# One rounding step of an attention kernel may run on GpSimd, and the written-out order behind the first batch is another one

## The chip, the cores and the metric

The kernel runs on one core of a Trainium2 chip. The metric is the time of one execution on the device in microseconds (us). A core has five engines with a queue of instructions each: TensorE (PE in the profile, its weight loads PEld), VectorE (DVE), ScalarE (ACT), GpSimd (POOL) and SyncE (SP), which here does nothing but issue DMAs. Each queue is worked off in order; engines wait for each other through semaphores.

## The reference

Block-causal attention over 8 batches with 8 heads, 576 tokens and 64 columns a head, then a two-layer feed-forward net with a relu6 gate:

```python
scores = scale * np.matmul(q, k.transpose(0, 1, 3, 2))          # q, k, v: (8, 8, 576, 64)
mask = block_i >= block_j                                        # blocks of 64 tokens
attn = exp(where(mask, scores, -1e9) - max); attn /= attn.sum() + 1e-9
x = (attn @ v).transpose(0, 2, 1, 3).reshape(4608, 512)
h = x @ w_in                                                     # 512 x 2048
g = h * np.clip(h + 3.0, 0.0, 6.0) / 6.0
out = g @ w_out                                                  # 2048 x 512
```

## The kernel before

**Numbers.** Behind the first batch every product is made of float16 words: a float32 value is split into a high word and a low word (the rest), and a product is three matmuls: high times high, high times low, low times high. So each intermediate needs two steps that round: one that writes the high word (`scaled`, on ACT or DVE), and one that computes value times scale minus high word (a `scalar_tensor_tensor` on DVE).

**Attention.** Two heads of a batch form a slot `n` (32 slots; 0 to 3 are the first batch, which is computed in float32). `qk_prep` splits q and k into the tile `qks`, and a transposing DMA brings it to `qkT`. `s_group(n, g)` does three blocks of 64 query rows: score matmuls into PSUM (`s`), a DVE step that moves them to `p` and takes the extreme value, the exponential on ACT, one divided by the sum in `st`, and then the split of P into the tiles `phl`. Query block `i` has 64 (i + 1) columns, so every block with an even `i` ends in a half block of 64 columns (five of nine blocks, 140 over slots 4 to 31). Where there are full columns besides, GpSimd first clears the other half of the last unit (`MEMSET p`). The high word of the half block goes into the left half of the last unit of `phl`, its low word into the right half. SP then issues a transposing DMA from `phl` to `pT` (five a slot), and the matmuls `pv` read `pT`.

**Feed-forward net.** 13 pieces of 384 tokens: `h` (x times w_in), relu6 and split into `g`, `o` (g times w_out). The last pieces use a seven-product scheme on half-size blocks: `w_comb` (tiles `wr`, `wq`, `ws`), `x_comb` (`xr`, `xt`) and `t_comb` (`tr`, `tw`) form sums and differences of the weights and of x, the products are `m`, and `g_pair` forms sums and differences of g in the tile `rs` and splits them into `gs` and `gr`, which the last `o` matmuls read. Sums and differences of `wr`, `xr`, `tr`, `tw` and `rs` may be done by DVE or by GpSimd.

**Order.** Nothing is scheduled when the kernel runs. The program is recorded as 6612 steps (`Recorder.add`, with the ways in which engines can do a step), and the table `ORDER` says in which order the steps are issued and on which engine each runs; `SLOTS` says which buffer of a pool each tile takes. `emit` plays the table, at one line for all engines: L423 before, L425 in the changed kernel.

Of the kernel before, what the change touches and what calls it, by code (L numbers as in the profile page):

```python
# [24 lines left out]
U = 2.211  # L25
# [58 lines left out]
    "%oBEx1`Qsn7?7C2QU(rmb#{wa(XnjzbcUrzT;r*er^gjO>DzDe<KQeIZ(hbzX;8A2yi_)9{Df@dip-{vi4ny`lSCzA375kcj2L-1"
    "yt!snN?zoU(PL&NrRuKaF3K+m3SOL+6Qv*97CmL<{#h}x#|*RU8>cF+wzMv3Dk~2?6BZJ>blLj$Yj9z%AFrrXTZeUYEmv!%byjWI"
    "xUaXmc4GJQIdwe^FQ(5RpW0Msd*Y<#*YC-v56pd7f8of{M}I!S#ku(S$-zUD{@yS%zZC!F^1P>*&u_ZppS_yDdyn?(%eSjn^{h!q"
    "tf^gVadVvw*0O=Q?e&ijtgTx%Z~tcXJ*oMpQpI-POQE&2PPx_g&Vyrzx4!$)v%lBy0WJjMxbc18Pw(SaI$_Yv+jj;J={NM=Fr2qG"
    "ynT6xD}BbS`?@nLR!+;!Ti_2xFv<qTC2)OL`S=Cs4J4}l&fY7DNduEp@^@V=C`_KWJ2Gm%vGYj!)Yxka7aYsHe)M>GT2WTTNKxgO"
# [1852 lines left out]
```

## Time and profile before

| | |
|---|---|
| runs | median 953.36 us (952.73 to 955.15, three runs) |
| the profiled execution | 951.95 us, its span 950.2 us |
| PE busy | 942.8 us of the span |
| DVE busy | 860.0 us |
| ACT busy | 722.0 us |
| POOL busy | 98.3 us |

An engine's busy time is the time in which its profiled instructions ran; the rest of the span it waited. The profiled execution's own time is 1.75 us above its span, which is what lies before the first and behind the last instruction.

### The profile page before, as it was taken

Reading aid. Unit: us, or ns where it says so; the run is one execution under the profiler, and the core shown is the slowest. Engines: PE = TensorE matmul, PEld = TensorE weight load, DVE = VectorE, ACT = ScalarE, POOL = GpSimd, SP = SyncE. Lnnn points to the kernel's source line nnn. Section 1 sums busy time; section 2 is a strip of 40 time slices with the busy share of each in tenths; the row PEclk is TensorE's granted clock in tenths of the full one; section 3 lists DMA queues with packets and bytes.
Section 4 is the critical chain, followed back from the end, with each engine's and each line's share of the span. In section 5 each row is a group of like instructions: output and inputs, shape, how many; then the busy total and the mean of one; then the engine's idle time right before and its main releaser. Section 6 shows DMA issues by size and latency. Waiting matters only on the chain.

```text
span 950.2 us, 34711 instructions
## 1 busy us (share of the span) xinstructions
PE 942.8 (99%) x14108; PEld 686.3 (72%) x14108; DVE 860.0 (91%) x2526; ACT 722.0 (76%) x1791; POOL 98.3 (10%) x283
## 2 busy tenths in 40 slices
PE   9999999999999999999999999999999999999998
PEld 7777777766677766666667666666666667789998
DVE  5988999999999999999999999999899998999987
ACT  6989898888988878888788878778665356676662
POOL 1443101100000000110000010100000102000000
PEclk9999999999999999999999999999999999999999
DMA  7877699989999999999999899986785000000001
GB/s 211 280 246 213 125 178 169 180 166 181 167 189 168 179 188 162 183 189 181 165 201 181 169 165 180 179 162 121 127 128 106 2 2 36 2 35 4 14 26 36
DMA packets 390704, 132.93 MB, mean 140 GB/s; under 512 B 373264, under 2 KB 376592, under 8 KB 390544
## 3 DMA queue, kind: packets, MB, share of 16 engines
q1 hardware_dynamic: 389456, 129.87, 71.7%
q8 instruction: 110, 1.80, 0.8%
q10 hardware_dynamic: 1088, 0.85, 0.3%
q14 instruction: 50, 0.41, 0.1%
HBM read 45.09 MB, written 9.44 MB: 57 GB/s over the span
## 4 chain that ended last, share of the span: by engine, by line
PE 97%; DMA 1%; DVE 1%; ACT 0%; issue 0%; SPq 0%; DVEq 0%
PE o L423 37%; PE h L423 30%; PE m L423 9%; PE s L423 7%; PE pv L423 6%; PE pf L423 1%; PE sf L423 1%; PE pt L423 1%; DMA qkT<-qks 1%; PE pr L423 1%; PE gm L423 0%; DMA qf<-in_q_dram 0%; PE warm L423 0%; PE o_1b L423 0%; PE o_2b L423 0%; PE o_0b L423 0%
## 5 line engine op out<-in xcount | busy, mean ns | idle before, releaser
L423 PE MATMUL o<-wout,g 128*64 128x512 f16 (+2 forms) x2760 | 346.5, 378 | 0.0
L423 PE MATMUL h<-x,win 128*64 128x384 f16 (+2 forms) x3568 | 330.1, 318 | 0.0
L423 PEld LDWEIGHTS <-win 128*64 128x64 f16 (+1 forms) x4432 | 231.7, 110 | 81.3 <-issue 1.7
L423 PEld LDWEIGHTS <-g 128*64 128x64 f16 x2784 | 154.0, 110 | 98.6
L423 DVE SCALAR_TENSOR_TENSOR phl<-p,st,phl 128x64 f16<-128x64 f32 (+4 forms) x364 | 154.9, 447 | 4.2 <-ACT phl L423 2.3
L423 ACT ACTIVATE p<-p,st 128x192 f32<-128x192 f32 (+8 forms) x252 | 139.1, 553 | 22.7 <-DVE st L423 20.7
L423 DVE CUSTOM_DVE_ANT_0 p<-s,none,esc 128x64 f32<-128x64 f32 (+7 forms) x252 | 119.9, 486 | 14.6 <-PE s L423 11.2
L423 ACT ACTIVATE r<-h,eg,sh 128x384 f32<-128x384 f32 (+1 forms) x176 | 101.5, 591 | 40.2 <-PE h L423 33.9
L423 ACT ACTIVATE phl<-p,st 128x512 f16<-128x512 f32 (+5 forms) x173 | 97.2, 582 | 11.2 <-DVE st L423 6.1
L423 PE MATMUL s<-qkT 128*64 128x512 f16 (+7 forms) x1120 | 98.5, 287 | 0.8 <-DMA qkT<-qks 0.8
L423 DVE SCALAR_TENSOR_TENSOR g<-r,g 128x384 f16<-128x384 f32 (+1 forms) x160 | 86.2, 546 | 3.8 <-ACT g L423 3.0
L423 DVE SCALAR_TENSOR_TENSOR r<-r,eg,h 128x384 f32<-128x384 f32 (+1 forms) x144 | 84.2, 586 | 5.8 <-ACT r L423 4.5
L423 ACT ACTIVATE g<-r 128x384 f16<-128x384 f32 (+1 forms) x117 | 58.3, 503 | 18.2 <-PE o L423 11.3
L423 PEld LDWEIGHTS <-qkT 128*64 128x64 f16 x1120 | 53.4, 110 | 25.1 <-DMA qkT<-qks 1.0
L423 PEld LDWEIGHTS <-vhl 128*64 128x64 f16 x1344 | 58.4, 110 | 13.4
L423 PE MATMUL pv<-pT,vhl 128*64 128x192 f16 (+2 forms) x1344 | 67.2, 233 | 0.0
L423 ACT ACTIVATE hf<-m 128x192 f32<-128x192 f32 x90 | 28.5, 327 | 36.9 <-PE m L423 31.9
L423 PEld LDWEIGHTS <-ws 128*64 128x64 f16 x1152 | 52.0, 110 | 4.1
L423 ACT ACTIVATION_READ_ACCUMULATOR p<-p,st 128x1 f32 x252 | 47.7, 189 | 0.0
L423 DVE SCALAR_TENSOR_TENSOR qks<-qk,rs_q,qks 128x576 f16<-128x576 f32 x56 | 46.8, 838 | 0.9 <-ACT qks L423 0.6
L423 PE MATMUL m<-x,ws 128*64 128x192 f16 x864 | 46.8, 246 | 0.0
L423 PE MATMUL m<-x,win 128*64 128x192 f16 x768 | 41.4, 246 | 0.4 <-DVE hf L423 0.4
(229 smaller groups left out, 1414.1 us busy)
## 6 DMA issues: line engine op xcount, KB each, us to landing
vx<-vhl SPq DMA_DIRECT2D x56, 160.0 KB, 3.4
vnat<-in_v_dram SPq DMA_DIRECT2D x63, 128.0 KB, 3.5
qk<-in_k_dram SPq DMA_DIRECT2D x28, 288.0 KB, 4.4
qk<-in_q_dram SPq DMA_DIRECT2D x28, 288.0 KB, 3.9
out_dram<-osb SPq DMA_DIRECT2D x29, 256.0 KB, 2.8
rawo<-in_moe_w_out_dram SPq DMA_DIRECT2D x13, 512.0 KB, 4.9
x<-in_moe_w_in_dram SPq DMA_DIRECT2D x9, 512.0 KB, 5.5
rawi<-in_moe_w_in_dram SPq DMA_DIRECT2D x6, 512.0 KB, 4.8
```

Of the source, the lines that this page charges most:

```text
L423: getattr(eng, method)(*args, **kw)
```

## The change

A new way for one step of `s_group`: the low word of a half block was one `scalar_tensor_tensor` on DVE; it may now also be two instructions on GpSimd, a `tensor_scalar` that multiplies the 64 columns of `p` in place by the scale, and a `tensor_tensor` that subtracts the high word. `ORDER` and `SLOTS` are other tables. Steps 0 to 899 of the order are as before, through the first batch; behind it the order differs throughout, and 503 of the 6612 steps run on another engine: 205 go from DVE to GpSimd (102 of the 140 low half blocks, the rest sums and differences), 144 from ACT to DVE, 109 from DVE to ACT, and 45 others.

```diff
--- before.py
+++ after.py
 ORDER = (
-    "c-l>Q1zaNC_qQS{Dvi0Rlyrl-X(u3IZra_oZrk0pZg+QgcXxMpcmL02pWpj=hvCLK-#GWqAk3~ghHbra)#^2C*O9O`!>rbC*obr4"
+    "c-lQ#1wb23(?$XT;t5)X2uX+=QpJKt30B43oht4wE!5rJ-QC^Y-Ch6L^!>k0xZRz3WOnazxwNKcuGp2UR<BvRj)buuVYz<8Mk}XH"
...
 )
 SLOTS = (
...
-    "Dmit$6EbYehQO3tn^m6AJKxerDn5LKB<*kJGQ7^&IkrmUwiEWL^LM6&x$xlkb>AM)%+2XL#wwB!+hKg<r2P*T{516+l#)KS><Op"
+    "=+LzJ%dIA&_PDK`eJZ+jkonGnRj+SWjo8hhITyMm!xr`VcmRARC!O+|O2*4OqkMW%u4F#9EfrTBeiWFBOGD6iJ^<nabCU^@"
 )
...
@@ -1153,9 +1155,14 @@
             else:
                 nc.scaled(ph[:, last, :BLK], pr[:, :BLK], r, "AV")
             if half:
-                nc.vector.scalar_tensor_tensor(
-                    ph[:, last, BLK:], pr[:, nk - BLK:nk], r, ph[:, last, :BLK], op0=ALU.mult, op1=ALU.subtract
-                )
+                ph_, pl, pw_ = ph[:, last, :BLK], ph[:, last, BLK:], pr[:, nk - BLK:nk]
+                nc.add([
+                    ("vector", "scalar_tensor_tensor", (pl, pw_, r, ph_), dict(op0=ALU.mult, op1=ALU.subtract)),
+                    ("gpsimd", [
+                        ("tensor_scalar", (pw_, pw_, r, 1.0), dict(op0=ALU.mult, op1=ALU.mult)),
+                        ("tensor_tensor", (pl, pw_, ph_), dict(op=ALU.subtract)),
+                    ]),
+                ])
             if g == 2:
                 nu = 2 * full + bool(half)
                 t_dma(pT[n, 1][:, BASE[i]:BASE[i] + nu], ph[:, :nu])
```

**GpSimd, behind the first batch.** These are the rows of GpSimd's queue where it first differs, before (a number behind a tile's name is slot and group or block: `p4_2` is block 2 of slot 4):

```order
L423 MEMSET p4_2_531 128x64
L423 MEMSET p4_4_552 128x64
L423 MEMSET phl4_1_555 128x128
L423 TENSOR_SCALAR qks5_541<-qks5_541 128x2x9x32 x2
L423 TENSOR_SCALAR st4_1_548<-st4_1_548 128x3
L423 MEMSET p4_8_582 128x64
L423 TENSOR_SCALAR qks6_609<-qks6_609 128x2x9x32
L423 TENSOR_SCALAR st4_2_577<-st4_2_577 128x3
```

And of the change:

```order
L425 MEMSET p4_2_531 128x64
L425 MEMSET p4_4_552 128x64
L425 MEMSET phl4_1_555 128x128
L425 TENSOR_SCALAR qks5_541<-qks5_541 128x2x9x32 x2
L425 TENSOR_SCALAR p4_2_531<-p4_2_531,st4_0_527 128x64
L425 TENSOR_TENSOR phl4_0_532<-p4_2_531,phl4_0_532 128x64
L425 TENSOR_SCALAR st4_1_548<-st4_1_548 128x3
L425 MEMSET p4_6_581 128x64
L425 TENSOR_SCALAR st4_2_577<-st4_2_577 128x3
L425 MEMSET p4_8_582 128x64
L425 TENSOR_SCALAR p4_8_582<-p4_8_582,st4_2_577 128x64
L425 TENSOR_TENSOR phl4_8_586<-p4_8_582,phl4_8_586 128x64
```

Behind the `MEMSET` of `p4_2` the low word of that block now stands as two rows, and block 8 follows; a `qks` step of slot 6 is gone from this place.

**DVE and GpSimd, late in the feed-forward net.** These are DVE's rows before around the sums `rs11_3` of piece 11 (`hf` is h of that group, `tr5` and `tw5` are combined weights that a later group needs):

```order
L423 SCALAR_TENSOR_TENSOR hf11_3_2392<-rs11_3_2395,eg8_698,hf11_3_2392 128x768
L423 SCALAR_TENSOR_TENSOR gs11_2_1_2391<-rs11_2_2388,gs11_2_1_2391 128x384
L423 TENSOR_TENSOR rs11_3_2395<-hf11_3_2392 128x192
L423 TENSOR_TENSOR hf11_4_2399<-m11_4_26_2401,hf11_4_2399 128x192
L423 TENSOR_TENSOR tr5_1_2344<-wout_86 128x512
L423 TENSOR_TENSOR hf11_4_2399<-m11_4_25_2400,hf11_4_2399 128x192
L423 TENSOR_TENSOR vnat_101<-tw4_2342,vnat_101 128x3x256
L423 TENSOR_TENSOR rs11_3_2395<-rs11_3_2395,hf11_3_2392 128x192
L423 TENSOR_TENSOR tw5_2345<-tr5_0_2343 128x256
L423 TENSOR_TENSOR hf11_4_2399<-m11_4_26_2401,hf11_4_2399 128x192
L423 SCALAR_TENSOR_TENSOR gr11_3_2396<-hf11_3_2392,gr11_3_2396 128x576
L423 TENSOR_TENSOR rs11_3_2395<-hf11_3_2392,rs11_3_2395 128x192
```

DVE's rows of the change at the same place:

```order
L425 SCALAR_TENSOR_TENSOR hf11_3_2392<-rs11_3_2395,eg8_698,hf11_3_2392 128x768
L425 TENSOR_TENSOR rs11_3_2395<-hf11_3_2392 128x192
L425 SCALAR_TENSOR_TENSOR gs11_2_0_2390<-rs11_2_2388,gs11_2_0_2390 128x384
L425 SCALAR_TENSOR_TENSOR gs11_2_1_2391<-rs11_2_2388,gs11_2_1_2391 128x384
L425 TENSOR_TENSOR hf11_4_2399<-m11_4_25_2400,hf11_4_2399 128x192
L425 TENSOR_TENSOR hf11_4_2399<-m11_4_26_2401,hf11_4_2399 128x192 x2
L425 TENSOR_TENSOR vnat_101<-tw4_2342,vnat_101 128x3x256
L425 SCALAR_TENSOR_TENSOR gr11_3_2396<-hf11_3_2392,gr11_3_2396 128x576
L425 SCALAR_TENSOR_TENSOR gs11_3_1_2398<-rs11_3_2395,gs11_3_1_2398 128x384
```

And GpSimd's of the change, of which before had none there:

```order
L425 TENSOR_TENSOR tr5_0_2343<-wout_86 128x512
L425 TENSOR_TENSOR tr5_1_2344<-wout_86 128x512
L425 TENSOR_TENSOR rs11_3_2395<-hf11_3_2392 128x192
L425 TENSOR_TENSOR rs11_3_2395<-rs11_3_2395,hf11_3_2392 128x192
L425 TENSOR_TENSOR rs11_3_2395<-hf11_3_2392,rs11_3_2395 128x192
L425 TENSOR_TENSOR tw5_2345<-tr5_0_2343 128x256
L425 TENSOR_TENSOR tw5_2345<-tr5_1_2344,tw5_2345 128x256
L425 TENSOR_TENSOR rs11_4_2402<-hf11_4_2399 128x192
L425 TENSOR_TENSOR rs11_4_2402<-rs11_4_2402,hf11_4_2399 128x192
L425 TENSOR_TENSOR rs11_4_2402<-hf11_4_2399,rs11_4_2402 128x192
```

One of the four `rs11_3` steps stays on DVE; three go to GpSimd, where they stand behind `tr5` and ahead of `tw5`.

**SP, at one transposing DMA.** These are SP's rows before that lead to `qkT13`:

```order
L423 DMA out_0_dram<-osb2_0_968 128x512
L423 DMA vnat_101<-in_v_dram 128x4x64 x2
L423 DMA_TRANSPOSE pT11_1_1022<-phl11_7_1031 128x8x128
L423 DMA vnat_101<-in_v_dram 128x4x64 x2
L423 DMA_TRANSPOSE pT11_1_1022<-phl11_8_1032 128x9x128
L423 DMA vnat_101<-in_v_dram 64x2x64
L423 DMA_TRANSPOSE qkT13_1069<-qks13_1062 128x27x128
```

And of the change:

```order
L425 DMA_TRANSPOSE pT11_1_1022<-phl11_6_1030 128x7x128
L425 DMA out_0_dram<-osb2_0_968 128x512
L425 DMA_TRANSPOSE pT11_1_1022<-phl11_8_1032 128x9x128
L425 DMA vnat_101<-in_v_dram 64x2x64
L425 DMA vnat_101<-in_v_dram 128x4x64 x2
L425 DMA_TRANSPOSE pT11_1_1022<-phl11_7_1031 128x8x128
L425 DMA_TRANSPOSE qkT13_1069<-qks13_1062 128x27x128
```

The transposing DMA of `qkT13` keeps its row number in the queue; what stands ahead of it changes places, and two DMAs fewer stand between the store of `osb2_0` and it.

## Rows read from the trace of the kernel before

**Rows 1.** The page: span, and busy time of each engine with its count.
```profile
span 950.2 us, 34711 instructions
...
PE 942.8 (99%) x14108; PEld 686.3 (72%) x14108; DVE 860.0 (91%) x2526; ACT 722.0 (76%) x1791; POOL 98.3 (10%) x283
```

**Rows 2.** Waits of PE: engine, tile, releaser; us in total, times, longest.
```profile
PE warm L423 <- DVE zero L423: 1.1, 1, 1.1
PE s L423 <- DMA qkT<-qks: 0.8, 1, 0.8
PE qt L423 <- DMA qf<-in_q_dram: 0.6, 1, 0.6
PE m L423 <- DVE hf L423: 0.4, 1, 0.4
```

**Rows 3.** Busy us by stretch (count): PE, PEld, DVE, ACT, POOL, clock, DMA.
```profile
0.00:50.00 50.00, 48.16 (x618) 36.70 (x619) 35.75 (x131) 38.55 (x110) 16.43 (x44) 1.00 0.76 242
...
150.00:700.00 550.00, 549.20 (x7704) 373.78 (x7702) 507.65 (x1586) 453.42 (x1165) 44.43 (x182) 1.00 0.98 171
700.00:830.00 130.00, 130.00 (x1908) 91.38 (x1906) 118.23 (x267) 73.11 (x153) 12.05 (x14) 1.00 0.21 41
830.00:930.00 100.00, 99.65 (x2286) 95.45 (x2284) 93.01 (x226) 64.13 (x142) 1.31 (x2) 1.00 0.06 19
930.00:950.20 20.20, 15.80 (x378) 15.54 (x373) 14.16 (x35) 2.95 (x6) 0.00 (x0) 0.95 0.15 42
```

**Rows 4.** Timeline of SP ahead of the wait for qkT: start, us.
```profile
293.01 1.54 SPq L423 DMA_TRANSPOSE pT<-phl  x1
294.60 0.67 SPq L423 DMA_DIRECT2D vnat<-in_v_dram  x1
295.37 5.07 SPq L423 DMA_TRANSPOSE qkT<-qks  x1
```

**Rows 5.** Timeline of PE at the same place: start, us.
```profile
298.35 0.91 PE L423 MATMUL pv<-pT,vhl 128*64 128x192 f16 x18
...
302.56 0.53 PE L423 MATMUL s<-qkT 128*64 128x64 f16 x12 [0.81 <-DMA qkT<-qks]
```

**Rows 6.** Groups by form, DVE and ACT: count, busy us, mean ns, idle before.
```profile
L423 DVE SCALAR_TENSOR_TENSOR g<-r,g 128x384 f16<-128x384 f32 x144 | 80.6, 567 | 2.8 <-ACT g L423 2.1
...
L423 ACT ACTIVATE g<-r 128x384 f16<-128x384 f32 x108 | 55.1, 515 | 15.7 <-PE o L423 9.7 <-DVE r L423 4.4 <-DVE st L423 0.9
...
L423 DVE SCALAR_TENSOR_TENSOR phl<-p,st,phl 128x64 f16<-128x64 f32 x140 | 39.2, 284 | 2.4 <-ACT phl L423 1.4
...
L423 DVE TENSOR_SCALAR g<-r 128x384 f16<-128x384 f32 x36 | 12.8, 354 | 1.2 <-PE mb_q L423 0.8
...
L423 DVE TENSOR_TENSOR rs<-hf 128x192 f32<-128x192 f32 x31 | 10.5, 353 | 0.2
```

**Rows 7.** Groups by form of POOL: count, busy us, mean ns, idle before.
```profile
L423 POOL TENSOR_SCALAR qks<-qks 128x576 f16<-128x576 f16 x26 | 20.9, 802 | 71.7 <-DVE qks L423 43.0 <-ACT qks L423 22.9 <-DVE pp L423 3.4
...
L423 POOL TENSOR_SCALAR st<-st 128x3 f32<-128x3 f32 x40 | 10.8, 271 | 230.7 <-ACT p L423 202.7 <-DVE r L423 12.6 <-issue 11.3
...
L423 POOL TENSOR_SCALAR sgi<-x 128x512 int32<-128x512 uint32 x9 | 6.6, 737 | 11.2 <-DVE win L423 3.3 <-DVE rsio L423 2.7 <-DVE wu L423 1.8
...
L423 POOL TENSOR_TENSOR tr<-wout 128x512 f32<-128x512 f16 x1 | 1.2, 1218 | 0.1
L423 POOL TENSOR_TENSOR tw<-tr,tr 128x256 f32<-128x256 f32 x1 | 0.7, 732 | 0.0
L423 POOL TENSOR_TENSOR rs<-hf 128x192 f32<-128x192 f32 x1 | 0.7, 712 | 110.9 <-DVE hf L423 110.9
```

**Rows 8.** Timeline of POOL and DVE at 744 us: start, us.
```profile
744.49 2.18 POOL L423 TENSOR_TENSOR wr<-win 128x1024 f32<-128x1024 f16 x1 [13.52 <-DVE wq L423]
744.71 2.37 DVE L423 SCALAR_TENSOR_TENSOR g<-r,g 128x384 f16<-128x384 f32 x1
```

**Rows 9.** DMA issues: count, us from issue to landing.
```profile
pT<-phl SPq DMA_TRANSPOSE x140, 4.2
```

More of the change, by code (lines that the diff above doesn't have):

```diff
@@ L84 @@
[L84 to L88, printed above, removed]
@@ new lines @@
+    "-HMgjjZHgxcdx47(?>7cnVhnE#>`m<7@Kxg<=nWwkGc2Yo42X^*Ke~sa{JCLdxv9-*Bm;&cJ`c`fANHGzrJrbIdk^G&k4WJ-Mx4J"
+    "o#|29!-<FOY|m3aUHCl7?8}vgtD7%x+4}5{z4^uTukWv=U9ubL^Zdn2-z7_zz4CtjgGBLH63Lzc83X5ju(I~E_p)(tbo%HZk;?ip"
+    "Pv9O689H1(C?TGu2pH__=o05n$GEc77#1F}O{Y$tE-84@f57C&L74)#dFf9jfk~FKQt61Y30dJQGMa-Y8j1=h35!KyE{De-HTtlo"
+    "rFKkmZp5&$<7OtNXs_ff%F7Q7TAZ34sT<!OHD%@gS<x}a^s^h9rpm9jwk>HcuLwC48XU58+4_!aaAK|>udE8ghIV!@4^vI=s@|}1"
+    "UvEv_#GdDK>Zdin=$k=4wW;3b#7Wh!-;+-tnESBd!jYqo{(ORybMf($gNG*ly<uW{DelYVc~8wgzv+p4_G<p_J?gJ7->zOYZB2Ya"
@@ new lines @@
+    "ZQWY)o9nDG7LCkpuYY`CZQZhY`!~z)i7h`B?yl^;6k2QBlw0lZJUBQ!_U=c|fnFmAIT45@W&Pjx^>ZnmFl6TKJ41&J7=CYrmA6{c"
+    "vAolnK4aE>?U@xTr|0A@@P{H8<%476xxTA>{FFL9iE6vE_ew(I;H2cdU03r9lIHD>h@2nZbtG+S%(aCJj%8dwdb}dFFtc*Buxi}c"
+    "G2@FiUfR4R%dNVmc++LWu&*h5_NIRmL|?c#inn^r_6OZ3*RDIUHR>^c-}l+VAE#0d96Y^a&fG(XfByRYXWQ^wf*UvAEPQ)={f57H"
+    "vTv3xzI*T8{Ra;p85WtbvTWa9&z>-e$LETc<P6H~@6>O=zzA1c<zQ!*C;L?<cA}-6OTLlfT8TI>zW^&8G4Ux|=4NBcbU%_=6JkX_"
+    "y6l++L-C1#vwUuiCl2-VB$01?IQIFY$Hu6U-W0pB@2(s_akB6QmFDL^WYCwZ*Is)03{`%R2W<9_Hh<+1Gpa6m^cefsjZK#WgEoyD"
@@ new lines @@
+    "ztv%T=C)u=Y-*YsKDg-_%{o1Ndh2hkpFG8JYDW2~+jrpF-qO-_`pnsi1+A42A3u0h71~gJc}Lr;4Po=no&WRK#I(I*Cf1DFIcrXT"
+    "t+kEjsri-J6DCf2Z$5eVh3+RMJ-BK3i$%qkFuQt>?zE!K@3WXP72`9I@N6IPwI$ZVbFSChJ$v^bczZb3^I-UqL&uJ1y&E*x^2Cs#"
+    "aoNKt-oppv<mS(CA(4HbzsW0je`?{P5ijD4rY9_h4^d%p`pXY#i64_@NTeqny{NRW-}ttrGI{yuFLoQ9ONVSw{3t1N`aW`T#ms*6"
+    "S!ylwr<Jum;}eU${MYZ)$_2BREVFlT_o!YW5LGRlv#4Gp)QP{<e0QBYFImrZ<1{t@_*u&{_$yc8Q_gSN96owVMC7meCjE#pEu>LV"
+    "zoW;DTfYU@K-d}(xOVJ7@|wDBQ~T|1>}qZ6UOKE}dC>HA2Uf#P?4sG}o&bu?-D#bF*00#Ga=?YZfkDCdLPEoapE*0?{sX6ny{7#?"
@@ new lines @@
+    "Zrn67n4X#SBs)iSPQ7QZvu6Ch9gOzAM^9fo({i}aH}8Mku+w$RwypZ@!p5fNFm|Ea%U!Qtzqy*57vl2v+B+uK?fnOpqtmC);f9vh"
+    ">o+35uyj05ba6gkAd$*DL<KQLp`&if6z*LSx5Vr3McwY)vFmGFd&-!dC8c-PjUQdMd&1cM;}R#%Px9C^Y02d7p7OP^cV1U4T~--a"
+    "Rb5m2G4)g3-RaXl4j4GdIX>Z&w@>ett9$qPj(S@^qi^Q^H?REC)0WR#@%7t*Ylp7SKD%<&ujGTD|E@lK<MET5x1O%~GUxWQqsJCx"
+    "$mDb9DcqmGuoxP>{eEs<{_x`uHb2@@Ff3;9)`cFPi|F5(THWs>Cr-M&Tzu|AA%kT)>W_)u?DP4eAK}!CD=vA_iV3!MUtA5RUq!4O"
+    "^3!~TkNH=B4BIk>XzxIt@Qw7W#q7+;Ro;|KSgXiWt8Lb7So_`A+V8nCptLFwS5jNo@Zx1?8U9u9w26~mPoC1&{`2>*eftj_#B_8u"
@@ new lines @@
+    "RtKeoMQz+LwMlinytTQa)1t<)vU^U?+(VX|X0B7m-9GWhBtGHtons;E#?8lCJ)E9;cQlWG@9E+3_h<FS&Jze1E=qgTZ_MI1N0u!0"
+    "^jfxDBp#cXlrp;S!GgDt8IqondChw0<CCY)ok?|YJnGbMeSa(KQ%_$1HGMeX{jlMhcUjqHkItXHa1m!NS1e9mvh>mim&@qlmPom>"
+    "cQ!UN2>9zaNJO`R&O9k!uxz<S@Zbf0me>(Dg#j3x#COG@D{VRTK_OvR$Be}jw{71M*xo_fxl1ITy_?Qpviw8Il#w3fTT~kC-Zf2U"
+    "SN9&J%JuyZHfP+`58mTr<MIn8mnScu(tkx^(SW@^D>23D#0gcaN*dw*rk!rDn-mpYF=~*Rx%>5)(WUzEju}&vCia$%pE+wbd@sZ&"
+    "EHp$!uD#e-SzU8!&hFE-b@dJB_FO){vggK`RTri;wVZ8MELsa2kahFcnyuTeT)lgJ^GCkm;Gr7}Rv*53Ywo;j^KZ9ibHh}7x9mG|"
@@ new lines @@
+    "^tM`~6^?L|960qdCs+5$^xo$$$A*i<lkT)`eDIL>=<(EV`%e!1{zFQfTz-G-&&oVmgWP>c<O2`SC&Qz>zCMjUequz-s41IL)1G<v"
+    "dp>gLuixnzn>OFP^`gRrLUqc_s;VC8J$lO@ADZo$I(@y*-x~I!t+kDVo1N|Kn-(nG=0azz_YL1LEQA?r&3UvvE<WMmy1g53@7THf"
+    "@soXi{z?bO{HMNt1%*ZaaRKoO`vVgX9!hE}9@i3Tc$Rp#gynj#wJoT<ps=GeI4L<I@5q6pcZ!ZV9l!s4*9+&|33rlHUW&83ay0Ov"
+    "6*Atv4=7EU*gbtdJt#!*(bA=C59`E95}DFNrA?dnfvL9*etTFMXkjS|bv<?ZEL+R@^riSSmlxjKH{;y-nX_>C3pZw8bQ6ltT({%f"
+    "ht2t_63zW~`AW&vQmmErHMLG{h-f#7j2<_B)abDjCOS;&pE^0MbBfLPA7wv(4KP)uXN>uM@4=&T$Cw>6XZ^{{+AWpI6$Aeclk9AY"
@@ L234 @@
+    "oxGN~E^51~uMus;v;ZC^QzxrCtK3Dj(HlmmNh6r8bnb+GSN;PMftApud(Ue!e+Rk1G%tNto<&<<_Lc`J-Wm4;)%vMiAEYbj24)1<"
+    "MW7seso$W9_s$k?y84aBe20-L=Ck1q^V?{*y?#rNcv%B-Dl@E|bp2%_K#`Dj(P=;z%e|K;-Q2|Tu*icsp7nQ3DXv>NWvrok{}^ZF"
+    "=+LzJ%dIA&_PDK`eJZ+jkonGnRj+SWjo8hhITyMm!xr`VcmRARC!O+|O2*4OqkMW%u4F#9EfrTBeiWFBOGD6iJ^<nabCU^@"
 )
```

262 lines of the change are left out of this document (118 added, 144 removed).

## The prediction

> **What bounds the kernel now.** I read the page first: PE is busy for 942.8 of 950.2 us, DVE for 860.0, ACT for 722.0, POOL for 98.3 [rows 1]. So PE sets the time, DVE is the next engine and POOL is nearly empty. The view of PE's waits comes second, because only what PE waits for can be saved. It lists four waits: 1.1 and 0.6 us at the start, 0.8 us for `qkT`, 0.4 us for `hf` [rows 2]. The windows then place the idle time: 1.84 us before 50 us, 0.80 between 150 and 700, nothing from 700 to 830, 0.35 from 830 to 930, and 4.40 in the last 20.2 us [rows 3]. The start is ordered as before (steps 0 to 899), and the last 20 us hold the drain of the last output block, on which no moved step bears. What a new order can still win from PE is therefore 0.80 + 0.35 = 1.15 us. The same windows show what slack DVE has: it is busy for 92.3% (507.65 of 550) between 150 and 700 us and for 93.0% between 830 and 930, and at that load PE still loses almost nothing [rows 3].
>
> **What is removed from DVE, and what comes.** 102 low words leave it at 284 ns: 29.0 us [rows 6]. Of the 205 steps that go to POOL, 45 are sums `rs` at 353 ns, 15.9 us [rows 6]; for the other some 58 (`tr`, `tw`, `wr`, `xr` and a few others) there is no DVE row of each kind, so I bound them by the cheapest DVE row here, 284 ns, and by POOL's own time for the dearest, 2.18 us, and take 0.5 us, near the low end since most are 512 columns or fewer: some 29 us. The other way, 144 steps come from ACT and 109 go to ACT. The dearest kind that comes is the high word of `g`, 19 steps, 354 ns on DVE against 515 on ACT: +6.7 us for DVE, −9.8 for ACT [rows 6]; the 16 other steps net I take at the same 354 ns, 6 us. DVE ends near 860 − 29 − 16 − 29 + 13 = 799 us, ACT some 10 to 20 us lower. None of this is PE's time: it is slack on engines that PE seldom waits for.
>
> **What comes to POOL.** The pair is in no row. Its `tensor_scalar` on 64 columns lies between 128x3 at 271 ns and 128x512 at 737; on the line between these, 271 + 61 × 466 / 509 = 327 ns [rows 7]. Its `tensor_tensor` lies below 192 columns at 712 ns and, as I bound it, above 271; the rows of 192 and 512 columns (712 and 1218) give 1.58 ns a column and so 712 − 128 × 1.58 = 510 ns [rows 7]. I take 0.84 us for the pair, bounds 0.54 to 1.04. That is 0.56 us more than the 284 ns on DVE (0.26 to 0.76). The sum on POOL: 102 × 0.84 = 86 us, 45 `rs` × 0.712 = 32, and for the other some 58 steps from 0.712 to 2.18, taken at 1 us, 58. POOL goes from 98 to some 270 of 950 us. It stays far from being the bound; what matters is how late a result of POOL may come.
>
> **How late a low word may come.** Behind it stand SP's transposing DMA into `pT` (4.2 us to land [rows 9]) and PE's `pv`. SP is a queue: a DMA that waits for POOL holds every load, store and transpose behind it, such as the transposing DMA of `qkT13`. At the one wait in this part the rows show the margin. The DMA of `pT` at 293.01 us lands 4.2 later, near 297.2, and the next `pv` begins at 298.35: some 1.1 us to spare [rows 4, 5, 9]. The 0.56 us fit in once, but not when POOL is in a `qks` step of 802 ns just then [rows 7]: 0.56 + 0.80 = 1.36, a quarter of a us too late. In such a place PE would wait some tenths of a us. The order moves `qks` steps off POOL at the place shown, and the wait of 0.81 us [rows 5] stands behind a transpose issued late, with a transpose and a load ahead of it in SP's queue [rows 4]. With fewer DMAs between the store and `qkT13`, I take this wait as gone. Cost of the low words on PE: nothing at the low end, since DMAs and `pv` of other blocks cover them; some tenths of a us in several places at the high end. I take one new wait of the size of the one seen, 0.8 us.
>
> **POOL beside DVE.** POOL's work is not free for DVE. While POOL ran a step of 2.18 us at 744.49, a DVE step `g` that takes 567 ns in the mean took 2.37 us and ended just behind it [rows 6, 8]: DVE stood still for about 1.8 us. The Trainium skill, page "SBUF — State Buffer", section "Who interferes with whom", says that a DVE instruction with two SBUF inputs and a GpSimd instruction that reads SBUF exclude each other for a whole instruction; this trace agrees, 2.37 us against 0.567 [rows 6, 8]. Between 150 and 700 us I count about 92 of the 102 pairs, by the share of the attention's slots there. DVE would be at 507.65 − 92 × 0.284 + 6.7 = 488.2 us of its own work. POOL's addition there is 92 × 0.84 = 77.3, less some 5 `qks` steps of 0.802: 73.3 us. If DVE stands still for none of it, it is busy for 488.2 of 550; for half of it, 524.9 (95.4%, against 92.3% before); for all of it, 561.5, which is 11.5 us more than there are. I take half, as a DVE step must be issued within POOL's and have the inputs for it. DVE then has less slack than before but is not the bound.
>
> **The sum.** The profiled execution took 951.95 us (950.2 and 1.75 around it); the median of the runs is 953.36, 1.41 above it. Forecast for a median: 951.95 + 1.41 − 1.15 + 0.8 = 953.0 us. If no new wait comes, 952.2. Both are inside 0.3% (2.9 us), about what a measurement of this kernel can tell from no change.
>
> **Rivals.**
> Slower, by DVE between 150 and 700 us: POOL holds DVE for more than half of its added time. It decides from (550 − 488.2) / 73.3 = 84%, where DVE is full; midway from there to all of it, 92%, DVE has 555.6 us to do and PE waits for 5.7: 951.95 + 1.41 + 5.7 = 959.1; at all of it, 964.9. For it: the 2.37 us [rows 8]. Against it: POOL's 44.43 us in that stretch let DVE get by before [rows 3], and a step beside POOL need not be held as long as the one at 744.71 us was [rows 8].
> Slower, by the sums `rs` between 795 and 930 us: PE waits for `gs`, whose split waits for `rs`. Three sums on POOL take 3 × (0.712 − 0.353) = 1.08 us more [rows 6, 7], and wait behind `tr` of 1.218 us twice [rows 7]. PE had one wait of 0.4 us there, for `hf` [rows 2], so little slack in one place at least. With 0.35 us in each of 16 groups: 5.6 us, and 951.95 + 1.41 − 0.8 + 5.6 = 958.2. It decides from nine groups, 3.1 us. Against it: the place shown has the high words read `rs` only after further products `m`, so the order leaves a group's time in between.
> Faster: PEld is busy for 95.45 of 100 us between 830 and 930 us [rows 3]. If matmuls there wait for weight loads in time that the profile shows as busy, an order that covers the loads better could win up to 99.65 − 95.45 = 4.2 us: 952.2 − 4.2 = 948.0 at best. It needs 3 of these 4.2. No row shows that such a wait exists.
> The change does nothing: the wait for `qkT` stays and nothing comes, 953.4. I count it with the forecast.
>
> **How the numbers follow.** Forecast 953.0, with the case that the wait stays: 0.56. The case without any new wait, 952.2: 0.14. DVE held by POOL, 959.1: 0.11. The sums late, 958.2: 0.11. Faster: 0.08. So faster 0.08, same 0.70, slower 0.22. The range reaches up to the points of both slower cases, 959.1 at most; below, to 952.2 less the 1 us by which single runs differ from each other (952.73 to 953.36 and 955.15): 951.2 to 959.1. It leaves out the upper halves of the slower cases (0.11) and most of the faster case (0.07). The likeliest case's own range is 952.2 to 954.8, with three more waits of 0.6.
>
> **What would show it.** Right: PE's idle time in the windows between 50 and 930 us stays under 2 us; no wait for `qkT` at 302 us; DVE's busy time from 150 to 700 us is 510 to 535 us though its steps are fewer; POOL's busy time is 230 to 290 us, the pair 0.54 to 1.04 us. Wrong for the DVE case: over 545 us in that window, and waits of PE that DVE ends. Wrong for the sums: waits of PE for `gs` or `o` in several groups between 800 and 930 us. Wrong altogether: SP waiting for POOL at many transposes, with waits of PE for `pT` or `qkT` of tenths of a us that sum to over 3 us; or matmuls of the same form with another mean duration.

## The result, and the profile after

The changed kernel takes 961.8 us (959.72 to 964.61, five runs), the kernel before 952.73 beside it. The ratio is 1.0094, with a 95% interval of 1.0068 to 1.0121: slower by about 9 us. The profiled execution has a span of 960.2 us, against 950.2 [rows 1]. The page:

```profile
span 960.2 us, 34948 instructions
...
PE 944.9 (98%) x14108; PEld 683.9 (71%) x14108; DVE 858.8 (89%) x2371; ACT 705.3 (73%) x1760; POOL 272.2 (28%) x567
```

With the same 14108 matmuls PE is busy for 2.1 us more, and it is idle for 15.3 us where it was idle for 7.4. POOL went from 98.3 to 272.2 us. DVE has 155 instructions fewer and the same busy time: that is the line to stop at. PE's waits, to be held against [rows 2]:

```profile
PE o L425 <- DVE g L425: 2.3, 2, 1.5
PE m L425 <- ACT hf L425: 2.0, 4, 1.1
PE qt L425 <- DMA qf<-in_q_dram: 1.8, 1, 1.8
PE m L425 <- DVE hf L425: 1.6, 2, 1.1
...
PE o L425 <- DVE gs L425: 0.3, 1, 0.3
PE o L425 <- DVE gr L425: 0.3, 1, 0.3
```

The wait for `qkT` is gone. New are waits that DVE and ACT end, for `g` and `hf`. The windows show where, in the columns of [rows 3]:

```profile
0.00:50.00 50.00, 46.99 (x611) 35.26 (x612) 34.74 (x128) 37.59 (x108) 15.64 (x43) 0.97 0.74 239
150.00:700.00 550.00, 549.68 (x7692) 368.80 (x7690) 499.77 (x1510) 448.56 (x1153) 122.15 (x359) 1.00 0.97 171
700.00:830.00 130.00, 128.01 (x1861) 93.59 (x1858) 123.23 (x255) 63.51 (x138) 38.84 (x37) 1.00 0.20 40
830.00:930.00 100.00, 95.19 (x2108) 89.02 (x2105) 89.56 (x158) 60.18 (x132) 60.47 (x67) 1.00 0.06 19
```

In the attention (150 to 700 us) PE is idle for 0.32 us, less than the 0.80 before. From 700 to 930 us it is idle for 6.80, against 0.35. In these 230 us DVE was busy for 211.25 us with 492 instructions before; now it is for 212.79 with 412. A mean instruction went from 429 to 516 ns. The granted clock is 1.00 there in both.

To see the loss without waits that hide in busy time, the matmuls of each trace were taken in order, each counted with the mean time of its form in the kernel before, and the times were compared at which equal sums of this work were reached. How much later than before the kernels of this study reach each point (us; the points are us of work; "late" is the last column less that at 690). Each row is one trace. Where the late part is that of the kernel before, in late_before and lows_only, the late column repeats to 0.01 us:

```
work             20     80    150    300    450    690    740    790    840    865    890    943   late
after          1.17   1.89   1.77   0.76   1.14   1.11   1.06   3.74   6.58   8.33   9.94   9.93   8.82
late_before   -0.04  -0.03  -0.19  -1.20  -0.84  -0.91  -0.91  -0.91  -0.91  -0.91  -0.91  -0.90   0.01
late_after    -1.29  -1.28  -1.38  -1.92  -1.92   4.27   4.21   6.89   9.73  11.51  13.08  13.06   8.79
lows_back      0.70   0.71   1.20   2.36   3.03   5.92   6.21   8.92  11.76  13.53  15.13  15.11   9.19
lows_only      0.08   0.20   0.06   1.70   1.72   3.77   3.75   3.78   3.77   3.77   3.77   3.77   0.00
b_sums         2.39   2.39   2.34   2.34   2.46   3.61   3.61   3.96   6.12   7.48   8.56   8.99   5.37
b_moves        1.38   1.38   1.76   1.59   1.59   2.21   3.60   4.25   5.06   5.06   5.96  10.23   8.02
b_engines      1.99   2.51   2.61   2.46   2.49   3.33   5.34   7.05  10.38  11.74  13.72  16.96  13.64
late_order    -0.12  -0.11  -0.33  -1.34  -0.49   0.64   3.94   8.33  10.04  10.66  14.86  17.61  16.97
moves_back    -1.60  -1.60  -1.56  -2.56  -1.36  -1.39   3.05  10.62  15.37  17.13  18.91  19.54  20.93
sums_back      1.20   1.22   1.30   0.30   0.96   0.93   0.87   2.29   2.26   2.85   7.31   8.36   7.44
rs_back        1.67   1.93   1.91   0.91   1.58   2.35   2.29   4.97   7.69  10.44  16.79  17.86  15.50
long_back     -0.78  -0.78  -0.70  -1.70  -0.80  -0.82  -0.88   0.53   1.68   2.63   4.43   4.42   5.24
wr_back        1.59   1.67   1.51   0.51   1.17   1.32   1.26   1.29   2.44   3.40   5.18   5.17   3.85
rs_only        0.02   0.02   0.23   0.65   0.65   0.61   0.55   0.58   0.56   0.58   2.98   2.96   2.36
b_twice       -1.58  -1.14  -1.07  -1.30  -1.29  -1.36  -1.36  -1.36   3.51  10.74  18.75  24.91  26.27
long_twice     0.26   0.37   0.25   0.54   1.61   2.39   3.35   9.04  12.38  16.43  20.86  20.86  18.47
```

The row `after`: 1.1 us are lost at the start, where the order is as before; the attention gives 0.8 back (1.89 to 1.11); then 8.8 us go between work 740 and 890, in the feed-forward pieces behind the attention. So neither the low words nor the order of the attention made the kernel slower. Ahead of step 900 order and engines are the same in all rows, and these starts lie between -1.60 and 2.39 us.

What happens there, in the timeline (start, us). GpSimd runs a sum `wr`, and beside it DVE does two steps `g`, 567 ns each [rows 6]:

```profile
773.61 2.25 POOL L425 TENSOR_TENSOR wr<-win 128x1024 f32<-128x1024 f16 x1 [3.08 <-DVE sh L425]
...
773.91 2.83 DVE L425 SCALAR_TENSOR_TENSOR g<-r,g 128x384 f16<-128x384 f32 x2
...
776.80 0.41 PE L425 MATMUL o<-wout,g 128*64 128x512 f16 x2 [0.83 <-DVE g L425]
```

They take 2.83 us instead of 1.13, and PE waits 0.83 us for the second. Sixty-five us later GpSimd runs two sums `tr`:

```profile
839.01 2.83 POOL L425 TENSOR_TENSOR tr<-wout 128x512 f32<-128x512 f16 x2
...
839.46 1.37 DVE L425 TENSOR_TENSOR tp<-tw,tp 128x512 f16<-128x512 f32 x1
...
840.75 1.30 DVE L425 TENSOR_TENSOR rs<-hf,rs 128x192 f32<-128x192 f32 x1
...
842.32 0.55 DVE L425 SCALAR_TENSOR_TENSOR g<-r,g 128x384 f16<-128x384 f32 x1
...
842.92 0.41 PE L425 MATMUL o<-wout,g 128*64 128x512 f16 x2 [1.51 <-DVE g L425]
```

The step `tp` takes 1.37 us (686 ns in the kernel before), `rs` 1.30 instead of 0.353 [rows 6], and PE waits 1.51 us for the `g` behind them. DVE's forms from 700 to 930 us before (busy, mean ns | idle):

```profile
L423 DVE TENSOR_TENSOR hf<-m,hf 128x192 f32<-128x192 f32 x69 | 23.5, 353 | 9.7 <-PE m L423 7.2 <-ACT hf L423 1.3 <-ACT gs L423 0.5
...
L423 DVE SCALAR_TENSOR_TENSOR gs<-rs,gs 128x384 f16<-128x384 f32 x27 | 14.8, 551 | 0.0
...
L423 DVE TENSOR_TENSOR rs<-hf 128x192 f32<-128x192 f32 x29 | 9.7, 353 | 0.2
L423 DVE SCALAR_TENSOR_TENSOR r<-r,eg,hf 128x384 f32<-128x384 f32 x16 | 9.7, 614 | 0.5 <-ACT r L423 0.4
...
L423 DVE TENSOR_TENSOR win<-tw,win 128x256 f16<-128x256 f32 x8 | 3.4, 420 | 0.0
```

And after:

```profile
L425 DVE TENSOR_TENSOR hf<-m,hf 128x192 f32<-128x192 f32 x66 | 21.7, 349 | 5.1 <-PE m L425 4.2 <-ACT hf L425 0.8 <-DVE win L425 0.2
...
L425 DVE SCALAR_TENSOR_TENSOR gs<-rs,gs 128x384 f16<-128x384 f32 x24 | 17.9, 754 | 2.1 <-ACT gs L425 2.0
...
L425 DVE SCALAR_TENSOR_TENSOR r<-r,eg,hf 128x384 f32<-128x384 f32 x16 | 11.8, 740 | 1.4 <-ACT r L425 1.4
...
L425 DVE TENSOR_TENSOR win<-tw,win 128x256 f16<-128x256 f32 x8 | 5.7, 719 | 0.0
L425 DVE TENSOR_SCALAR g<-r 128x384 f16<-128x384 f32 x12 | 5.4, 453 | 0.3
...
L425 DVE TENSOR_TENSOR rs<-hf 128x192 f32<-128x192 f32 x9 | 4.9, 556 | 0.1
```

`hf<-m,hf`, which has one input in PSUM (`m`) and one in SBUF, is as long as before, 349 against 353 ns. The four other forms of the first list, with both inputs in SBUF, are 21 to 71% longer. That is what [rows 8] showed once: a DVE step stands still while GpSimd runs one, called the hold from here on. The Trainium skill, page "SBUF — State Buffer", section "Who interferes with whom", makes this distinction, between a DVE instruction with two SBUF inputs and one with at most one outside its 2-port perf modes; the trace agrees (353 and 349 against 420 and 719). Two SBUF inputs are not all: `g<-r`, with one, went from 354 [rows 6] to 453 ns.

The same can be counted step by step. Take what each DVE step adds to DVE's busy time, less the mean of the same form in the kernel before where no GpSimd step runs beside it. Behind 700 us, the 182 DVE steps of the changed kernel that run beside a GpSimd step took 42.2 us more than that, and the 274 others 0.6. In the kernel before it is 4.8 us for 25 steps, and 0.4 for the others. Forty-seven of the 182 are `hf<-m,hf`, and they took no more than alone. So DVE's own work behind 700 us fell by 28.4 us, from 219.7 to 191.3, and the hold rose by 37.4: some 9 us more in sum, about as much as the late loss.

### The profile page after: what moved, and what is told of

Same layout as the page of the kernel before. It is cut to its first block, busy times and chain, and to the rows that moved or that the text cites. A ratio compares the mean times of both kernels' runs of the same rounds, so it can differ in the third digit from the quotient of the medians.

```text
span 960.2 us, 34948 instructions
## 1 busy us (share of the span) xinstructions
PE 944.9 (98%) x14108; PEld 683.9 (71%) x14108; DVE 858.8 (89%) x2371; ACT 705.3 (73%) x1760; POOL 272.2 (28%) x567
## 5 line engine op out<-in xcount | busy, mean ns | idle before, releaser
L425 PEld LDWEIGHTS <-win 128*64 128x64 f16 (+1 forms) x4432 | 228.9, 110 | 82.6 <-issue 1.2
L425 ACT ACTIVATE p<-p,st 128x64 f32<-128x64 f32 (+8 forms) x252 | 139.1, 553 | 24.3 <-DVE st L425 22.9
L425 DVE SCALAR_TENSOR_TENSOR phl<-p,st,phl 128x384 f16<-128x384 f32 (+4 forms) x262 | 131.8, 517 | 3.6 <-ACT phl L425 2.0
L425 POOL TENSOR_SCALAR p<-p,st 128x64 f32<-128x64 f32 x102 | 52.3, 513 | 240.5 <-ACT phl L425 147.6
L425 ACT ACTIVATE phl<-p,st 128x384 f16<-128x384 f32 (+5 forms) x166 | 94.2, 586 | 16.8 <-issue 5.4
L425 PE MATMUL s<-qkT 128*64 128x64 f16 (+7 forms) x1120 | 99.3, 287 | 0.0
L425 ACT ACTIVATE g<-r 128x384 f16<-128x384 f32 (+1 forms) x100 | 48.8, 496 | 12.9 <-DVE r L425 6.2
```

The costliest lines, as they stand in the source:

```text
L425: getattr(eng, method)(*args, **kw)
```

## The experiments

Theory A, after the result: the loss is made in the late pieces by the sums on GpSimd. Rival B: it comes from the low half blocks or the order of the attention and only shows late. Rival C: the late order itself. Rival D: the late moves between ACT and DVE. Two bytes of `ORDER` hold a step's number and its engine, so that order and engines can be exchanged apart; the edits below are of that table if nothing else is shown.

| kernel | median, us | ratio to before, 95% interval |
|---|---|---|
| late_before | 953.3 | 1.0006, 0.9994 to 1.0019 |
| late_after | 964.76 | 1.0124, 1.0105 to 1.0144 |
| sums_back | 960.42 | 1.0078, 1.0061 to 1.0096 |
| lows_back | 966.57 | 1.0143, 1.0122 to 1.0164 |
| b_sums | 959.63 | 1.0081, 1.0061 to 1.0102 |
| late_order | 971.15 | 1.0200, 1.0176 to 1.0224 |
| b_moves | 961.82 | 1.0095, 1.0073 to 1.0116 |
| b_twice | 979.1 | 1.0281, 1.0259 to 1.0303 |
| long_back | 957.65 | 1.0059, 1.0037 to 1.0082 |
| rs_back | 967.65 | 1.0165, 1.0145 to 1.0185 |
| moves_back | 975.14 | 1.0227, 1.0206 to 1.0249 |
| b_engines | 966.03 | 1.0145, 1.0123 to 1.0167 |
| wr_back | 955.54 | 1.0038, 1.0023 to 1.0054 |
| rs_only | 955.33 | 1.0032, 1.0018 to 1.0045 |
| lows_only | 957.71 | 1.0060, 1.0040 to 1.0080 |
| long_twice | 972.27 | 1.0197, 1.0174 to 1.0221 |

### Which part of the program

**late_before**: the changed kernel up to step 5050, then the order and engines before.

```diff
 ORDER: steps 0 to 5049 of the changed kernel
-ORDER: steps 5050 to 6611 of the changed kernel
+ORDER: the same steps in the order and on the engines of the kernel before
```

> The order and engines of the changed kernel for the first 5050 of 6612 steps (all of the attention but its end, with the low half blocks on GpSimd), and those of the kernel before for the rest. Theory A (the loss is made in the last feed-forward pieces): 951 to 954 us, as the kernel before. Rival B (the low half blocks on GpSimd, or the order in the attention, delay something that shows only later): 960 to 963 us, as the changed kernel.

**late_after**: the reverse.

```diff
-ORDER: steps 0 to 5049 of the changed kernel
+ORDER: steps 0 to 5049 of the kernel before
 ORDER: the rest in the order and on the engines of the changed kernel
```

> The reverse: the first 5050 steps as in the kernel before (low half blocks on DVE), the rest in the order and on the engines of the changed kernel. Theory A: 960 to 963 us, the whole loss. Rival B: 951 to 954 us. If the loss needs both parts, something between in both kernels.

**lows_back**: `ORDER` of the changed kernel, the 102 low half blocks on DVE.

```diff
-lows_back: 102 low half blocks on gpsimd
+lows_back: 102 low half blocks on vector
```

> The changed kernel with the 102 low half blocks back on DVE and everything else as it is. Theory A: 960 to 964 us, no gain. Rival B: 953 to 956 us.

**lows_only**: `ORDER` of the kernel before, the 102 low half blocks on GpSimd.

```diff
-lows_only: 102 low half blocks on vector
+lows_only: 102 low half blocks on gpsimd
```

> The kernel before with nothing changed but the 102 low half blocks on GpSimd. If the pair is hidden in any order: 951 to 954 us. If the order of the attention had to be made for it: 955 us or more, with waits of PE for pT.

late_before, with 96 of the 102 low half blocks on GpSimd, is as fast as the kernel before, and its late column is 0.01. late_after has the whole late loss, 8.8 us, and some 6 us ahead of 690, most of it at the seam, where two orders that do not fit meet: between 680 and 690 us PE waits 2.0 us for DVE, and the granted clock is 0.83 there in the mean of its two levels (1.2 and 2.4 GHz). It and lows_back came out above both forecast ranges. So rival B is out. lows_back is slower than the changed kernel: in this order the low words on GpSimd save the attention some 5 us. And lows_only shows that they are not free by themselves: in the order before they cost 3.6 us, all before 690, in PE's waits

```profile
PE pv L419 <- DMA pT<-phl: 2.5, 2, 2.0
...
PE s L419 <- DVE x L419: 0.5, 1, 0.5
...
PE s L419 <- DMA qkT<-qks: 0.3, 1, 0.3
```

which fits the forecast's late low word ahead of SP's transposing DMA: at the longest wait, SP issues the transposes at 249.44 us, just behind a low word that GpSimd ended at 249.27, and PE goes on at 255.53. It is the order of the attention that hides them.

### Which part of the late pieces

All of these have one of the two orders throughout, and late steps on other engines.

**sums_back**, **moves_back**, **late_order**: the order of the changed kernel.

```diff
 ORDER: order of the changed kernel
-late engines of the changed kernel
+sums_back:  95 steps rs, tr, tw, wr, xr as before
+moves_back: the 64 other late changes as before
+late_order: all 159 as before
```

> The changed kernel with the 95 sums and differences rs, tr, tw, wr, xr that changed engines put back on the engine that they had before (93 of them from GpSimd to DVE); the order of the steps is that of the changed kernel. Theory A in its narrow form (these sums on GpSimd are the loss): 952 to 956 us, the wait of PE in the last pieces falling from 6.8 us to under 3. Rival C (the order of the late steps, or the moves between ACT and DVE, are the loss, whichever engine does the sums): 960 us or more, since DVE then has some 45 us more to do in an order that was not made for it.

> The changed kernel with the 64 other late changes of engine undone (mostly between ACT and DVE; DVE is relieved by some 9 us), the sums on GpSimd, its order kept. If these moves overfill DVE: 953 to 957 us. If the order of the changed kernel needs them, as late_order suggests: 964 us or more.

> The order of the changed kernel throughout, but every step of the late part (behind step 5050) on the engine that it had before: sums on DVE, and the 64 moves between ACT and DVE undone. Rival C (the late order itself): 958 to 962 us, as with only the sums put back. Rival D (in that kernel the moves from ACT to DVE were what kept PE waiting, on top of sums on DVE): 952 to 955 us.

**b_sums**, **b_moves**, **b_engines**: the order before, with the late engines of the changed kernel for the 95 sums, for the other 64 steps, and for all 159.

```diff
 ORDER: order of the kernel before
-late engines of the kernel before
+b_sums:    95 steps rs, tr, tw, wr, xr as in the changed kernel
+b_moves:   the 64 other late changes as in the changed kernel
+b_engines: all 159 as in the changed kernel
```

> The order of the kernel before throughout, low half blocks on DVE, and only the 95 sums and differences rs, tr, tw, wr, xr on the engines of the changed kernel (93 of them on GpSimd). Theory A (a sum on GpSimd is too slow or holds DVE, wherever it stands in the order): 958 to 964 us, with waits of PE behind DVE and ACT in the last pieces. Rival C (the late order of the changed kernel is the loss): 952 to 955 us.

> The order of the kernel before throughout, and in its late part only the 64 other changes of engine of the changed kernel (mostly between ACT and DVE); the sums stay on DVE. Rival D: 956 to 962 us, since DVE gets more than it gives. Theory A: 952 to 955 us, within 0.3% of the kernel before.

> The order of the kernel before, with all 159 late changes of engine (sums on GpSimd and the other 64). If the losses of these parts add (5.4 us for the sums and 7.4 for the rest behind 700 us, measured one by one in this order): 963 to 967 us. If the sums pay for the moves (one takes from DVE what the other gives): 953 to 957 us, and the late order is what remains of the loss.

Each part costs something. In the order before, the sums cost 5.4 us late, the moves 8.0, both 13.6: they add. In the changed order, undoing the sums helps by 1.4 us only, and undoing the moves makes it worse, 20.9 against 8.8; with all 159 undone it is 17.0, and 971.15 us is above both ranges forecast for late_order. So the narrow form of theory A missed: with the sums on DVE again, PE waits nearly as much, behind `hf` instead of `g`:

```profile
PE m L419 <- ACT hf L419: 4.4, 6, 1.6
...
PE m L419 <- DVE hf L419: 1.4, 2, 1.2
```

So late order and late engines go together, and neither can be judged by undoing the other. What a sum on GpSimd costs has to be looked for at the sums themselves.

### Hold or lateness

Theory L: the sums cost by holding DVE while they run, above all the long ones. Theory R: `rs` comes late.

**b_twice**: the kernel before, DVE with all its work; 83 sums are done again on GpSimd, into a tile that nobody reads.

```diff
             for method, args, kw in o.ways[o.eng]:
                 getattr(eng, method)(*args, **kw)
+            if o.n in TWICE:
+                (method, (out, a, b), kw), = o.ways["gpsimd"]
...
+                    self.nc.gpsimd.tensor_tensor(w, x, y, **kw)
```

> The kernel before, with DVE doing all its work, and 83 of the sums (rs, tr, tw) done a second time by GpSimd into a tile that nobody reads. Extra work; the output's values are untouched. Nobody waits for a result of GpSimd here, so only what GpSimd's running does to others is left. If GpSimd holding DVE is the price: DVE's busy time grows by some 20 us behind 750 us and the kernel takes 957 to 963 us. If the price is that results of GpSimd come late: 952 to 955 us, DVE's steps about as long as before.

**long_back**: in the changed kernel, 13 `tr` and 5 `wr` on DVE again. **wr_back**: these and the two `wr` and one `tr` that were on GpSimd before too. **rs_only**: all `tr`, `wr`, `tw`, `xr` on DVE, only `rs` on GpSimd. **rs_back**: only the sums `rs` as before.

```diff
 ORDER: order of the changed kernel
-long_back: 18 steps tr, wr on gpsimd
+long_back: 18 steps tr, wr on vector
-wr_back: 21 steps tr, wr on gpsimd
+wr_back: 21 steps tr, wr on vector
-rs_only: 54 steps tr, wr, tw, xr on gpsimd
+rs_only: 54 steps tr, wr, tw, xr on vector
-rs_back: 47 steps rs as in the changed kernel
+rs_back: 47 steps rs as in the kernel before
```

> The changed kernel with the 18 long sums (13 tr, 5 wr, 1.4 and 2.3 us each on GpSimd) back on DVE. Theory L (GpSimd's long steps hold DVE, and PE waits for the DVE step behind): the three waits of PE at 776.8, 788.3 and 842.9 us (0.83, 1.10 and 1.51 us) go, 957.5 to 959.5 us. Theory R (what costs is that rs comes late): no change, 960.5 to 963 us.

> The changed kernel with all 21 sums tr and wr on DVE (with the two wr and one tr that the kernel before had on GpSimd). If the wait of 1.19 us that is left at 785 us (PE behind DVE hf, behind a step xt that took 2.01 us while GpSimd's last wr ran) is the hold too: 1.2 us less than with 18 of them, about 956.5 us. If not: 957 to 959 us.

> The changed kernel with all sums tr, wr, tw, xr on DVE, and only rs on GpSimd. Theory L for the rest (tw at 0.9 us hold DVE as well): 954 to 956 us. If what is left is the order, made for tw on GpSimd: 957 to 962 us, since DVE gets some 13 us more.

> The changed kernel with the sums rs (46 go back to DVE, one the other way) on the engines of the kernel before. Theory R: the waits of PE behind ACT hf and gs from 845 us on go, 957 to 959 us. Theory L: 961 to 964 us, since the long steps still hold DVE and DVE gets 16 us more.

**long_twice**: long_back, and GpSimd does the 18 again, as in b_twice.

> The kernel of the run with the 18 long sums back on DVE, and GpSimd does these 18 a second time, in pieces of 256 columns, into a tile that nobody reads. Nobody waits for these results. Theory L (it is the hold that costs): 960 to 966 us, the waits behind held DVE steps come back, DVE's busy time grows by some 10 us. If it is the lateness of the results: 957 to 959 us, as without.

b_twice lost more than either theory said, 26.3 us. No result of GpSimd is used, so none is late. DVE's forms in it, from 700 to 930 us:

```profile
L422 DVE TENSOR_TENSOR hf<-m,hf 128x192 f32<-128x192 f32 x58 | 19.6, 348 | 4.2 <-ACT hf L422 3.8 <-PE m L422 0.3
...
L422 DVE TENSOR_TENSOR rs<-hf 128x192 f32<-128x192 f32 x22 | 10.4, 485 | 0.1
```

Again `hf<-m,hf` is untouched (353 before), `rs` goes from 353 to over 480 ns. Over the whole program the same 2526 DVE steps take 30 us more, against 860.0 [rows 1]:

```profile
PE 951.1 (98%) x14108; PEld 695.6 (71%) x14108; DVE 890.0 (91%) x2526; ACT 721.4 (74%) x1791; POOL 177.1 (18%) x379
```

In one window DVE has almost nothing left:

```profile
830.00:930.00 100.00, 83.87 (x1712) 76.78 (x1710) 96.07 (x176) 50.79 (x112) 57.59 (x70) 0.95 0.04 13
```

It is busy for 96.07 of 100 us, against 93.01 [rows 3], and PE is idle for 16.13; the clock granted to it is 0.95 there in the mean, against 1.00 [rows 3], which is a part of the loss, by estimate some 5 us at most (0.05 of 100). Not all of it need be the hold: the second sums also read `hf` and `rs`, whose buffers are then free later (behind 700 us one wait of ACT for GpSimd comes by it, 3.3 us). PE's waits in this kernel are for DVE in the main: 8.4 us for `hf`, 3.6 for `gr`, 0.9 for `gs`.

long_back met theory L: 3.6 us less late, and the two waits shown above are gone. The third that was to go, 1.10 us at 788.3, stayed: it stands beside a `wr` that GpSimd had before too and that was not among the 18 (start, us):

```profile
782.11 2.50 POOL L420 TENSOR_TENSOR wr<-win 128x1024 f32<-128x1024 f16 x1 [37.56 <-DVE wq L420]
...
782.81 2.01 DVE L420 TENSOR_TENSOR xt<-xr,xt 128x192 f32<-128x192 f32 x1
...
785.14 0.60 PE L420 MATMUL m<-vnat,ws 128*64 128x192 f16 x10 [1.19 <-DVE hf L420]
```

`xt` takes 2.01 us (352 ns before), beside the last `wr`. wr_back takes it away: from 740 to 790 us of work it loses nothing. rs_only takes `tw` and `xr` off as well, and 2.4 us of the 8.8 are left. What this last step gave is read from one trace each; the medians of wr_back and rs_only are the same (955.54 and 955.33):

```profile
PE m L420 <- ACT hf L420: 2.0, 3, 1.2
...
PE o L420 <- DVE gr L420: 0.2, 1, 0.2
```

long_twice is the control: the results come from DVE in time, GpSimd's 18 steps run for nothing, and the late loss goes from 5.2 to 18.5 us; 972.27 us is above both ranges. DVE's busy time grows by 17.6 us against long_back, from 855.6 to 873.2. Its rows at the place of the second timeline above, where GpSimd does the two `tr` again in four pieces:

```profile
844.46 3.41 POOL L432 TENSOR_TENSOR halves<-wout 128x256 f16<-128x256 f16 x4
...
844.90 0.89 DVE L423 TENSOR_TENSOR tp<-tw,tp 128x512 f16<-128x512 f32 x1
...
845.71 0.82 DVE L423 TENSOR_TENSOR rs<-hf,rs 128x192 f32<-128x192 f32 x1
846.45 0.89 DVE L423 TENSOR_TENSOR win<-tw,win 128x256 f16<-128x256 f32 x1
...
847.27 1.02 DVE L423 SCALAR_TENSOR_TENSOR g<-r,g 128x384 f16<-128x384 f32 x1
...
848.34 0.41 PE L423 MATMUL o<-wout,g 128*64 128x512 f16 x2 [1.49 <-DVE g L423]
```

The four DVE steps take 3.62 us; `rs` alone goes from 353 to 820 ns, `win` from 420 to 890, and the wait of 1.51 us that long_back had lost is back with 1.49. Nobody waits for these four pieces. In this kernel `rs` and `tw` also wait behind the extra steps in GpSimd's queue, so a part of the 13.2 us may be lateness; in b_twice nobody waits for GpSimd's results, apart from the one wait of ACT for a buffer, and it lost as much and more. So the hold can make such a loss without late results. rs_back is the other side: bringing `rs` back to DVE in the changed order loses 6.7 us more, again above both ranges. `rs` on GpSimd (0.70 us) is a relief there, `tr` and `wr` (1.39 and 2.28) are not:

```profile
L425 POOL TENSOR_SCALAR p<-p,st 128x64 f32<-128x64 f32 x102 | 52.3, 513 | 240.5 <-ACT phl L425 147.6 <-DVE phl L425 57.0 <-ACT am_q L425 10.4
L425 POOL TENSOR_TENSOR phl<-p,phl 128x64 f16<-128x64 f32 x102 | 41.4, 406 | 8.5
L425 POOL TENSOR_TENSOR tr<-wout 128x512 f32<-128x512 f16 x14 | 19.4, 1394 | 12.7 <-ACT hf L425 6.5 <-DVE xt L425 3.4 <-DVE tw L425 2.8
...
L425 POOL TENSOR_TENSOR wr<-win 128x1024 f32<-128x1024 f16 x7 | 16.0, 2283 | 33.4 <-DVE wq L425 30.3 <-DVE sh L425 3.1
...
L425 POOL TENSOR_TENSOR rs<-hf 128x192 f32<-128x192 f32 x22 | 15.4, 700 | 30.0 <-DVE hf L425 30.0
```

## Why the prediction was wrong

- **The pair and its cover.** Right, and not what decided. The pair took 0.513 + 0.406 = 0.92 us (forecast 0.84, bounds 0.54 to 1.04); POOL came to 272.2 us (forecast some 270). The wait for `qkT` went, and 0.32 us of idle time remain between 150 and 700 us (0.8 forecast for a new wait). That PE need not pay for it held only in the new order: in lows_only it paid 3.6 us.
- **POOL beside DVE in the attention.** Mis-sized, on the safe side. I took half of the 73.3 us that POOL was to gain there as lost to DVE, 524.9 us busy; measured 499.77. Counted step by step as above, the hold from 150 to 700 us is 7.4 us, against 5.5 before: 2 us more, not 37. The first slower rival, priced for this stretch, did not come.
- **The step that failed**: "POOL's work is not free for DVE" was worked out for 150 to 700 us alone, while 93 of the 205 steps that go to POOL are the sums behind 700 us (102 are low words, and ten are neither), where DVE was already busy for 92% and I saw only "slack on engines that PE seldom waits for". I counted these sums off DVE's time, some 45 us, without what they take from it. From 700 to 930 us DVE's time did not fall: 211.25 to 212.79. Over the whole program DVE came to 858.8 us instead of the forecast 799: its own work fell by 43 us, not 61, and its steps beside GpSimd's took 38 us more than in the kernel before, 37 of them behind 700 us.
- **The rival for the sums** had the right stretch and, for most of the loss, the wrong mechanism: lateness of `rs`, 0.35 us in each of 16 groups, with waits for `gs`. No run shows the 16 groups. The waits for `gs` and `gr` are 0.3 us each, and rs_back shows `rs` on GpSimd as a gain. The rival's 958.2 us was 3.6 too low. A late `rs` did reach PE once, by way of ACT's `hf`, for 1.15 us; that `rs` took 1.40 us on GpSimd, where its form has 0.78 in the mean:

```profile
860.59 1.40 POOL L425 TENSOR_TENSOR rs<-hf,rs 128x192 f32<-128x192 f32 x1
...
862.02 0.55 ACT L425 ACTIVATE hf<-m 128x192 f32<-128x192 f32 x2 [1.53 <-POOL rs L425]
...
862.40 0.69 PE L425 MATMUL m<-x,ws 128*64 128x192 f16 x12 [1.15 <-ACT hf L425]
```
- **What is shown.** Taking the steps `tr`, `wr`, `tw` and `xr` off GpSimd brings the late loss from 8.8 to 2.4 us, and running 18 of them idle brings it up by 13. As the steps go, the hold behind 700 us goes from 42.2 us to 24.9 (long_back), 20.5 (wr_back) and 8.7 (rs_only), and the late loss from 8.8 to 5.2, 3.8 and 2.4. So the hold is the larger part. Each sum put back is also work for DVE again: from wr_back to rs_only the hold falls by 12 us, DVE's own work rises by as much, from 207.7 to 219.7, and the medians do not differ. The last 2.4 us (work 865 to 890, PE behind ACT `hf`) stay open between `rs` on GpSimd and the late order. The 1.1 us at the start arise where order and engines are as before, and not from the change.

No kernel here beats the one before: late_before, with the low words on GpSimd and the late part as it was, is the best, and the same. PE bounds both.

## What to carry to other kernels

A sum moved from DVE to GpSimd is paid twice: by its own time there, and by the DVE steps that meet it, those with two SBUF inputs above all. Price it by the longest GpSimd step and by what DVE runs beside it, in the stretch where it lands. Where DVE has no slack, move short steps. Long ones might be put beside DVE steps that read PSUM, which were not held here; no run tried it. And price a moved step in the order that it will run in: the same 102 low words cost 3.6 us in one order and nothing in the other.

## What was not expected of the hardware

- In the attention the pair on GpSimd hardly holds DVE: the form `phl<-p,st,phl` of 128x512 took 754 ns from 150 to 700 us before and 759 after. GpSimd is the one that waits, it seems: its `tensor_scalar` took 0.32 us at a quiet place of lows_only and 0.469 in the mean there. Why these short steps wait and the long sums hold, no run shows.
- In 16 of the 18 profiles PE waits for the DMA of `qf` at the start, for 0.4 to 2.8 us, though the first 900 steps are the same. The starts differ for more reasons than this wait: late_after waits 1.3 us, 0.7 longer than the kernel before, and is 1.29 us ahead of it at work 20. What else differs stays open. It is why the table above is read by differences along a row.
